# Twelve blocks of w2 in one half of the partitions and ten in the other: dealing the last MLP's units unevenly

## The chip, the cores and the metric

The kernel runs on one core of a Trainium2 chip. The metric is the device time of one execution in microseconds. A core has five engines that run side by side and wait for one another by semaphores: TensorE (PE; its weight loads are shown apart as PEld), VectorE (DVE), ScalarE (ACT), GpSimd (POOL) and SyncE (SP), which here issues nearly all transfers. Transfers between the chip's main memory and the on-chip memory of 128 partitions are carried out by 16 DMA engines.

## What is computed

One decoding step of a small transformer, in float32: two layers, each an attention block over a cache and an MLP, with the same weights and caches in both.

```python
def _A_ref(x, k_cache, v_cache, wq, wo):       # H=32 heads, Sk=4096, Dh=128, D=512
    q = (x @ wq).reshape(B, Sq, H, Dh).transpose(0, 2, 1, 3)
    scores = jnp.einsum("bhqd,bhkd->bhqk", q, k_cache) * (Dh ** -0.5)
    p = _softmax(scores, axis=-1)
    o = jnp.einsum("bhqk,bhkd->bhqd", p, v_cache)
    return o.transpose(0, 2, 1, 3).reshape(B, Sq, H * Dh) @ wo

def _B_ref(x, w1, b1, w2, b2):                 # D=512, F=1376
    h = _gelu(jnp.einsum("bsd,df->bsf", x, w1) + b1)
    return jnp.einsum("bsf,fd->bsd", h, w2) + b2

x = A_x
x = x + _A_ref(_layernorm(x), A_k_cache, A_v_cache, A_wq, A_wo)
x = x + _B_ref(_layernorm(x), B_w1, B_b1, B_w2, B_b2)
x = x + _A_ref(_layernorm(x), A_k_cache, A_v_cache, A_wq, A_wo)
x = x + _B_ref(_layernorm(x), B_w1, B_b1, B_w2, B_b2)
```

There is one token (B = Sq = 1). Every weight and both caches have to be read from main memory, 286 MB in all, and each element is used once a layer.

## The kernel before

**Storage.** One large tile, `arena` (L71), holds all weights and cache pieces. It is cut by hand into three regions for K or V of one group (`RING`, `A_AT`, `B_AT`, `C_AT`, L37) and some smaller places. `U` is 512 columns, `NC` 2,048. The heads are worked off in eight groups (`G`) of four. A group's K and V are 8 blocks of `NC` columns each, 8 MB each.

**Order of the work.** Layer one takes the groups 0 to 7 (loop at L417), layer two takes them backwards (L514). For each group, `blocks` (L353) issues the load of K, PE takes the scores, `exponentials` and `weights` make the softmax, V is loaded and multiplied. In the groups before the last, PE multiplies the first three blocks of V and `weighted` (L261) lets DVE multiply the other five and add them up in a tree (L265 and L270), in place, in columns 12U to 32U of the region that holds V. The tree's second addition (L270, 128x2048) is the last to read columns 20U to 24U.

**Queues.** All loads are issued by SP through `load` (L105), which keeps them in program order: an issue that has to wait for its place to become free, or for an earlier transfer's semaphore, holds those behind it. PE's matmuls are kept in program order as well (L110).

**The end.** The last group (L514 with `final`) has its V in region B. While it is worked on, region A, which held V of the group before, takes the MLP's weights. SP issues, in this order: V in four pieces (`LAST`, L53), the last quarter of wo (L528), w1 in three pieces (`W1_AT_END`, L52) to A_AT, and w2 in four pieces (`W2_AT_END`, L55: blocks 0 to 3, 4 to 7, 8 and 9, 10) to A_AT + 11U. Then `head_out` multiplies by wo and `mlp` (L307) does the rest.

**The MLP.** The 1,376 hidden units are dealt to four strips of 32 partitions, 344 each (`FJ`). For each chunk `c` of the input, four matmuls, one a strip, multiply by w1 (L310 to L313) into the PSUM tile `pO`. A few small steps take the norm. `idle(pS)` (L322) is a matmul whose result is not used, but for zeroing. DVE transposes `pO` in 32 x 32 squares (L324), so that the units stand in the partitions: strip j's unit 32 c + q comes to partition 32 j + q, column c. There are `FB` = 11 such columns, the last padded with zeros. Then come the GELU's steps (L326 to L333) on 11 columns, and for each column c four matmuls multiply block c of w2 (512 columns, 128 partitions) and add up in `pS` (L334 to L337). After one more transpose and addition SP stores the output (L538). Layer one's MLP is the same function, with its own order of w2's loads (`load_w2`, `behind_w2`). The bias b1 comes with a small transfer at the start, on ACT's queue (L131).

Of the kernel before, what the change touches and what calls it, by code (L numbers as in the profile page):

```python
# [14 lines left out]
ALU = mybir.AluOpType  # L15
AX = mybir.AxisListType

P = 128
# [4 lines left out]
J = 4  # L23
C = 8
FJ = F // J
FB = 11
W1C = FJ * J
EPS = 1e-5
U = 512
# [8 lines left out]
A_AT, B_AT, C_AT = RING  # L38
KEPT_V = 26 * U
SHARED = B_AT + KEPT_V  # L40
SCRATCH = SHARED + 10 * U
# [10 lines left out]
W1_AT_END = ((0, 2), (2, 3), (3, 4))  # L52
LAST = ((0, 4), (4, 6), (6, 7), (7, 8))  # L53
W2_AT_CHANGE = ((0, 2), (2, 5), (5, 8), (8, 10), (10, 11))
W2_AT_END = ((0, 4), (4, 8), (8, 10), (10, 11))  # L55


@with_exitstack
def decode_layers(ctx: ExitStack, tc: tile.TileContext, vectors, k, v, w, w1, w2, out):
    nc = tc.nc  # L60
    const = ctx.enter_context(tc.tile_pool(name="const", bufs=1))
    psum = ctx.enter_context(tc.tile_pool(name="psum", bufs=1, space=bass.MemoryType.PSUM))
# [19 lines left out]
    def small(name, n=1):  # L82
        nonlocal first_front, rest
        if name.startswith("gelu_"):
            i = "huaztg".index(name[-1])
            return cells[:, gelu + FB * i : gelu + FB * (i + 1)]
        if name not in places:
            fit = [j for j in range(J) if gaps[j] + n <= ends[j]]
            if name == "by_dma":
                places[name] = front, first_front, n  # L90
                first_front += n
            elif fit:
                places[name] = cells, gaps[fit[0]], n
                gaps[fit[0]] += n
            else:
                places[name] = cells, rest, n
                rest += n
        t, a, m = places[name]
        assert m == n and first_front <= FRONT and rest <= CELLS
        return t[:, a : a + n]  # L100

    def at(first, n):
        return arena[:, first : first + n]

    def load(first, src):  # L105
        t = at(first, src.shape[-1])
        tc.keep_in_program_order(nc.sync.dma_start(t, src))  # L107
        return t

    def matmul(*a, **kw):  # L110
        tc.keep_in_program_order(nc.tensor.matmul(*a, **kw))  # L111
# [4 lines left out]
    def part(src, g, a, b):  # L116
        return src[g][:, NC * a : NC * b]

    def of_w(row, i, n):
        return w[row][:, NC * i : NC * (i + n)]  # L120

    def by_four(t):
        return t.rearrange("p (j n) -> p j n", j=4)
# [6 lines left out]
    b1c, b2c, xcol = by_dma[:, :FB], by_dma[:, FB : FB + 4], by_dma[:, FB + 4 :]  # L130
# [12 lines left out]
    pS, pO = (psum.tile([P, 512], F32, name=n) for n in ("pS", "pO"))  # L143
# [10 lines left out]
    def of_32(t, n, i=0):  # L154
        return t[:, : 32 * n].rearrange("p (c q) -> p c q", q=32)[:, :, i]
# [4 lines left out]
    def pairs(t):  # L160
        return t[:, :8].rearrange("p (c i) -> p c i", i=2)
# [32 lines left out]
    def mean_of(xs, s):  # L194
        nm = minus_mean(s, pS[:, 0:1])
        xc, sq, ss, negm = small("xc", 4), small("sq", 4), small("ss"), small("negm")
        nc.vector.tensor_scalar(xc, pairs(xs)[:, :, 0], nm, None, op0=ALU.add)
        nc.vector.scalar_tensor_tensor(sq, xc, 1.0, xc, op0=ALU.mult, op1=ALU.mult, accum_out=ss)
        nc.vector.tensor_copy(negm, nm)
        return negm, ss  # L200

    def rstd_of(ss):
        nv = minus_mean(ss, pS[:, 1:2])
        ve, r = small("ve"), small("rstd")
        nc.vector.tensor_scalar(ve, nv, -1.0, EPS, op0=ALU.mult, op1=ALU.add)
        nc.vector.memset(pS[:, 0:2], 0.0)
        nc.gpsimd.tensor_tensor(r, ve, power, op=ALU.pow)
        return r
# [95 lines left out]
            else:  # L304
                matmul(to, on[:, d : d + P], wt[:, d, :], start=(d == 0), stop=(d == 3))

    def mlp(xs, s, w1_t, w2_t, load_w2=None, behind_w2=None):  # L307
        xb = small("xb", 4)
        nc.gpsimd.tensor_tensor(xb, pairs(xs)[:, :, 0], b2c, op=ALU.add)
        for c in range(4):  # L310
            for j in range(J):
                matmul(pO[32 * j : 32 * j + 2, :FJ], pairs(xs)[:, c, :], w1_t[c][:, FJ * j : FJ * (j + 1)],
                       start=(c == 0), stop=(c == 3))  # L313
            if c == 0:
                nm, ss = mean_of(xs, s)
            if c == 1:
                r = rstd_of(ss)
            if load_w2:
                load_w2(c)
                for _ in range(min(c + 1, 2) if c < 3 else 0):  # L320
                    idle(pO[:, 3 * P :], P, amid=True)
        idle(pS)  # L322
        ht = at(SCRATCH, 32 * FB)
        nc.vector.transpose(ht, pO[:, : 32 * FB])  # L324
        h, u, a, z, t, g = (small(f"gelu_{i}", FB) for i in "huaztg")
        nc.vector.scalar_tensor_tensor(h, of_32(ht, FB, 1), nm, of_32(ht, FB), op0=ALU.mult, op1=ALU.add)  # L326
        if load_w2:
            load_w2(4)
        nc.vector.scalar_tensor_tensor(u, h, r, b1c, op0=ALU.mult, op1=ALU.add)
        nc.vector.scalar_tensor_tensor(a, u, 0.044715, u, op0=ALU.mult, op1=ALU.mult)  # L330
        nc.vector.scalar_tensor_tensor(z, a, 1.0, u, op0=ALU.add, op1=ALU.mult)
        nc.scalar.activation(t, z, AF.Tanh, scale=float(np.sqrt(2.0 / np.pi)))
        nc.vector.scalar_tensor_tensor(g, t, 1.0, u, op0=ALU.add, op1=ALU.mult)  # L333
        for c in range(FB):  # L334
            for j in range(J):
                matmul(pS[32 * j : 32 * j + 1, :P], g[:, c : c + 1], w2_t[c][:, P * j : P * (j + 1)],
                       start=(c == 0), stop=(c == FB - 1))  # L337
            if load_w2:
                behind_w2(c)
                if c in (4, 7, FB - 1):  # L340
                    idle(pO, U // 2)
        return of_32(turned(pS), 4), xb

    def load_w1(first, a, b):
        load(first + W1C * a, w1[:, W1C * a : W1C * b])

    def load_w2(first, a, b):
        load(first + U * a, w2[:, U * a : U * b])

    def in_rows(first, n, rows):  # L350
        return [at(first + n * i, n) for i in range(rows)]

    def blocks(src, g, home, pieces=((0, C),)):  # L353
        for a, b in pieces:
            load(home + NC * a, part(src, g, a, b))
            for c in range(a, b):
                yield c, quarters(home + NC * c)

    xs, s = set_x(zero, 1.0, xcol)
# [54 lines left out]
    negm, z, sc, nsc = first_queries(xs, s, wq_t, wide=True)  # L414
    acc = pairs(xs)[:, :, 0]
    ahead = None
    for g in range(G):  # L417
        final = g == G - 1
        k_home, v_home = RING[2 * g % 3], RING[(2 * g + 1) % 3]
# [4 lines left out]
        if g < G - 2:  # L424
            t = partly(pt, blocks(v, g, v_home), v_home)
            pair = load(PAIR, of_w(g % 2, g, 2))
            ahead = t, rl, by_four(pair[:, :NC])
            z = next_queries(xs, negm, by_four(pair[:, NC:]), to=pS)
            continue
        for c, t in blocks(v, g, v_home, LAST if final else ((0, C),)):  # L430
# [3 lines left out]
            if g == G - 2:  # L434
                for j in range(J):
                    i = 4 * c + j - KEPT_V // U
                    if i >= 0:
                        nc.scalar.copy(pK[i], t[j])
        if final:
# [3 lines left out]
            own = head_out(rl, wo_t, last=True, home=ident)  # L443
            load_w1(SHARED, 3, 4)
        else:
# [3 lines left out]
            z = next_queries(xs, negm, wq_t)  # L449
    x1, s1 = set_x(own, 1.0, acc, queries=False)  # L450
# [9 lines left out]
    def behind_w2(c):  # L460
# [4 lines left out]
        if c == 9:  # L465
            begin_k(SHARED + 2 * NC, 2)

    own, xb = mlp(x1, s1, in_rows(SHARED, W1C, 4), in_rows(SHARED, U, FB),
                  lambda i: load_w2(SHARED, *W2_AT_CHANGE[i]), behind_w2)
    xs, s = set_x(own, 0.5, xb)  # L470

# [3 lines left out]
    g = G - 2  # L475
    negm, z, sc, nsc = first_queries(xs, s, wq_t)
# [22 lines left out]
    v_t = [at(B_AT + U * i, U) for i in range(KEPT_V // U)]  # L499
    for i, first in enumerate([SHARED, SHARED + U] + [PAIR + U * j for j in range(4)]):  # L500
        t = at(first, U)
# [8 lines left out]
    z = next_queries(xs, negm, by_four(pair[:, :NC]))  # L510
# [3 lines left out]
    for n in range(2, G):  # L514
        g, final = G - 1 - n, n == G - 1
        k_home, v_home = homes[(2 * n - 1) % 3], homes[2 * n % 3]
        acc, pt, rl = group(z, acc, ahead, blocks(k, g, k_home, HALVES if final else ((0, C),)))
        if not final:
            t = partly(pt, blocks(v, g, v_home, ((0, 6), (6, 8)) if n == 2 else ((0, C),)), v_home)
            pair = load(PAIR, of_w(g % 2, g - 1, 2))  # L520
            ahead = t, rl, by_four(pair[:, NC:])
            z = next_queries(xs, negm, by_four(pair[:, :NC]), to=pS)
            continue
        for c, t in blocks(v, g, v_home, LAST):
            values(c, pt, t, c)
            if c in (5, 7):
                idle(pS)
        wo_t = by_four(load(PAIR, of_w(g % 2, g, 1)))  # L528
        for a, b in W1_AT_END:
            load_w1(A_AT, a, b)  # L530
        for a, b in W2_AT_END:
            load_w2(A_AT + 11 * U, a, b)
        own = head_out(rl, wo_t, last=True)
    x1, s1 = set_x(own, 1.0, acc, queries=False)
    own, xb = mlp(x1, s1, in_rows(A_AT, W1C, 4), in_rows(A_AT + 11 * U, U, FB))
    y = small("y", 4)
    nc.vector.scalar_tensor_tensor(y, own, 0.5, xb, op0=ALU.mult, op1=ALU.add)
    nc.sync.dma_start(out, y)  # L538
# [2 lines left out]
def columns(a):  # L541

    return np.ascontiguousarray(a.reshape(J, 4, 32, -1).transpose(0, 2, 1, 3).reshape(P, 4, -1))
# [36 lines left out]
```

## Time and profile before

| | before |
|---|---|
| median of 3 runs | 673.12 us (673.02 to 673.5) |
| profiled run | 673.93 us, its span 672.1 us |
| mean granted TensorE clock | 0.794 |
| PE busy | 400.7 us (60% of the span) |
| DVE busy | 329.1 us (49%) |
| moved by DMA | 285.98 MB, mean 425 GB/s |

The span runs from the first to the last event of the program in the profile; the run's own time has a little more around it. A profile is one execution. In its rows, "idle before <- releaser" tells how long an engine had stood still and what ended that. A DMA share of 1 is all 16 engines at work; it can read a little above 1 where neighbouring packets overlap. PE's clock is granted by a throttle, 1.00 or 0.50. A matmul in float32 is recorded as two instructions. For an issued transfer the time "to landing" runs from the issue on SP to the last increment of its semaphore.

### The profile page before, as it was taken

The page shows a single profiled execution, that of the slowest core. Times are in us where ns is not written, and L with a number is a line of the kernel's source. Part 1 is how long each engine was busy: PE and PEld are TensorE (multiplying, and loading weights), DVE is VectorE, ACT ScalarE, POOL GpSimd, SP SyncE. Part 2 cuts the span into 40 slices and gives each one's busy share as a digit, 9 for nine tenths or more (in the row PEclk, how much of TensorE's full clock was granted, in tenths as well). Part 3 has the DMA queues.
Part 4 walks back from the last instruction along what each step waited for, and adds up shares of the span by engine and source line. Part 5 has one row for each costly group of instructions (what it writes and reads, how often), then busy time and mean ns, then how long its engine had stood idle before and what let it go on. Part 6 is the DMA issues. An engine that isn't in the chain of part 4 may idle for free. (4 is left out here: it accounts for less than half of the span.)

```text
span 672.1 us, 5792 instructions
## 1 busy us (share of the span) xinstructions
PE 400.7 (60%) x2470; PEld 109.8 (16%) x2470; DVE 329.1 (49%) x480; ACT 22.8 (3%) x48; POOL 4.9 (1%) x23
## 2 busy tenths in 40 slices
PE   4543753647616556376767878728527466275685
PEld 1110210111201111011214222102102111021122
DVE  2059276393682945921121221492772936928521
ACT  0010000000000000002000110000000000000000
POOL 0000000000000000000000000000000000000000
PEclk9956765976769767677989999877758867687698
DMA  9999999999999999999999999999999999999996
GB/s 375 437 437 437 438 430 437 414 456 437 437 434 410 459 434 437 433 434 395 433 423 393 426 452 421 437 435 434 437 433 409 458 434 430 437 426 419 435 420 257
DMA packets 11258, 285.98 MB, mean 425 GB/s; under 512 B 1505, under 2 KB 1505, under 8 KB 3297
## 3 DMA queue, kind: packets, MB, share of 16 engines
q1 hardware_dynamic: 11088, 285.61, 98.9%
q8 instruction: 19, 0.31, 0.2%
q14 instruction: 7, 0.05, 0.0%
q10 hardware_dynamic: 144, 0.01, 0.0%
HBM read 285.62 MB, written 0.00 MB: 425 GB/s over the span
## 5 line engine op out<-in xcount | busy, mean ns | idle before, releaser
L111 PE MATMUL pO<-arena,cells 128*128 128x512 f32 (+4 forms) x376 | 93.0, 606 | 145.5 <-DVE arena L270 127.7
L111 PE MATMUL pS<-arena,front 128*8 128x512 f32 x1036 | 146.4, 706 | 32.8 <-DMA arena<-in_k 29.1
L265 DVE TENSOR_TENSOR arena<-arena 128x10240 f32<-128x10240 f32 x11 | 119.1, 10825 | 32.0 <-DMA arena<-in_v 31.8
L111 PE MATMUL pO<-arena 128*4 128x512 f32 x584 | 94.7, 806 | 44.7 <-DMA arena<-in_v 42.9
L270 DVE TENSOR_TENSOR arena<-arena 128x2048 f32<-128x2048 f32 (+1 forms) x33 | 98.5, 2985 | 0.7
L228 DVE TENSOR_REDUCE cells<-pS 128x1 f32<-128x512 f32 x16 | 11.1, 692 | 152.1 <-PE pS L111 152.1
L111 PEld LDWEIGHTS pO<-arena,cells 128*128 128x128 f32 (+3 forms) x376 | 28.2, 122 | 195.1 <-DVE arena L270 136.8
L111 PEld LDWEIGHTS pS<-arena,front 128*8 128x8 f32 x1036 | 31.4, 101 | 154.0 <-issue 110.3
L111 PE MATMUL pS<-arena,cells 128*1 128x128 f32 (+1 forms) x328 | 50.5, 384 | 8.5 <-DMA arena<-in_w 7.0
L280 DVE STREAM_TRANSPOSE arena<-pO 128x512 f32<-128x512 f32 x16 | 11.5, 717 | 54.1 <-PE pO L111 54.1
L242 PE MATMUL pO<-front,arena 128*128 128x128 f32 x64 | 12.8, 333 | 36.9 <-ACT arena L237 36.9
L111 PEld LDWEIGHTS pO<-arena 128*4 128x4 f32 x584 | 16.2, 102 | 107.7 <-issue 99.8
L169 DVE STREAM_TRANSPOSE arena<-pO 32x128 f32<-32x128 f32 x64 | 19.9, 311 | 20.1 <-PE pO L111 19.1
L237 ACT ACTIVATE arena<-pS,cells 128x512 f32<-128x512 f32 x16 | 12.4, 778 | 502.8 <-DVE cells L233 502.8
L111 PEld LDWEIGHTS pS<-arena,cells 128*1 128x1 f32 (+1 forms) x328 | 21.9, 118 | 45.2 <-issue 36.4
L231 DVE TENSOR_REDUCE cells<-cells 128x1 f32<-128x8 f32 x16 | 2.6, 161 | 29.4 <-PE pO L111 29.2
L242 PEld LDWEIGHTS pO<-front,arena 128*128 128x128 f32 x64 | 8.1, 161 | 49.9 <-ACT arena L237 48.8
L169 DVE STREAM_TRANSPOSE arena<-pS 32x128 f32<-32x128 f32 x44 | 13.7, 310 | 0.8
L171 DVE STREAM_TRANSPOSE arena<-pS 128x128 f32<-128x128 f32 x3 | 1.0, 317 | 12.7 <-PE pS L111 12.7
L247 DVE STREAM_TRANSPOSE cells<-cells 128x32 f32<-128x32 f32 x16 | 3.4, 214 | 7.0 <-ACT arena L237 5.9
L384 DVE MEMSET pS<- 128x512 f32 x11 | 5.3, 485 | 1.2
L245 DVE COPY arena<-pO 128x128 f32<-128x128 f32 x16 | 4.5, 284 | 1.4 <-PE pO L242 1.1
(63 smaller groups left out, 73.6 us busy)
## 6 DMA issues: line engine op xcount, KB each, us to landing
arena<-in_w SPq DMA_DIRECT2D x13, 2048.0 KB, 11.5
arena<-in_k SPq DMA_DIRECT2D x4, 4096.0 KB, 25.1
arena<-in_v SPq DMA_DIRECT2D x2, 4096.0 KB, 38.9
arena<-in_w SPq DMA_DIRECT2D x6, 1024.0 KB, 21.4
arena<-in_v SPq DMA_DIRECT2D x3, 2048.0 KB, 43.0
arena<-in_v SPq DMA_DIRECT2D x1, 6144.0 KB, 30.8
arena<-in_w SPq DMA_DIRECT2D x6, 688.0 KB, 30.3
arena<-in_v SPq DMA_DIRECT2D x4, 1024.0 KB, 46.2
```

What stands on the lines that cost most here:

```text
L111: tc.keep_in_program_order(nc.tensor.matmul(*a, **kw))
L169: nc.vector.transpose(t[q], src[q, P * j : P * (j + 1)])
L228: nc.vector.tensor_reduce(ml[:, 0:1], pS, axis=AX.X, op=ALU.max)
L231: nc.vector.tensor_reduce(m, mt[:, :C], axis=AX.X, op=ALU.max)
L237: nc.scalar.activation(p, pS, AF.Exp, bias=bias[:, 0:1], scale=sc, accum_out=ml[:, 0:1])
L242: tc.keep_in_program_order(nc.tensor.transpose(pT[:, b].rearrange("p j r -> p (j r)"), p[:, P * b : P * (b + 1)], ident))
L245: nc.vector.tensor_copy(pt, pT[:, :, :, :C].rearrange("p b j c -> p c j b"))
L247: nc.vector.transpose(lt, ml)
L265: nc.vector.tensor_tensor(t, t, w.unsqueeze(2).to_broadcast([P, 4 * J * (C - BY_PE), P]), op=ALU.mult)
L270: nc.vector.tensor_tensor(a, a, b, op=ALU.add)
L280: nc.vector.transpose(ot, pO)
L384: nc.vector.memset(pS, 0.0)
```

## The change

It touches the last MLP only; layer one's MLP is called with values that leave it as it was.

- The units are dealt 384, 384, 304 and 304 to the four strips (`UNITS_AT_END`). After the transpose the partitions under 64 have twelve columns of units, the others nine and a half, padded to ten. A second copy of w2, `w2_at_end`, is laid out for that, with twelve blocks a row; blocks 10 and 11 are loaded and multiplied for the partitions under 64 alone.
- All 128 partitions load blocks 0 to 9, in four pieces (0 to 3, 4 to 6, 7 and 8, 9). Blocks 10 and 11 of the lower 64 partitions come in eight transfers of eight rows, four partitions apart (3, 7, ... 31, say), 4,096 bytes a row, 32 KB a transfer. Three of them are issued between and behind the pieces of V, one behind wo, three behind w1's pieces and one behind w2's first piece.
- w2's blocks are multiplied in the order 10, 11, 0, 1, ... 9, and for 10 and 11 with 64 rows.
- w1 gets 64 columns in front, of which the first twelve hold b1 in the new dealing; so it comes with w1's first piece.
- The GELU's small arrays lie in region A of the arena, not in `cells`, and have twelve columns.

```diff
-W2_AT_END = ((0, 4), (4, 8), (8, 10), (10, 11))
+W2_AT_END = ((0, 4), (4, 7), (7, 9), (9, 10))
+UNITS_AT_END = (384, 384, 304, 304)
+FB_AT_END, FB_BOTH = 12, 10
+HEAD = 64
...
-    def mlp(xs, s, w1_t, w2_t, load_w2=None, behind_w2=None):
+    def mlp(xs, s, w1_t, w2_t, units, n, b1c, gelu_at, load_w2=None, behind_w2=None):
...
-                matmul(pO[32 * j : 32 * j + 2, :FJ], pairs(xs)[:, c, :], w1_t[c][:, FJ * j : FJ * (j + 1)],
+                a = sum(units[:j])
+                matmul(pO[32 * j : 32 * j + 2, : units[j]], pairs(xs)[:, c, :], w1_t[c][:, a : a + units[j]],
                        start=(c == 0), stop=(c == 3))
...
-        for c in range(FB):
+        first = 0 if load_w2 else FB_BOTH
+        for i in range(n):
+            c = (first + i) % n
+            rows = w2_t[c].shape[0]
             for j in range(J):
-                matmul(pS[32 * j : 32 * j + 1, :P], g[:, c : c + 1], w2_t[c][:, P * j : P * (j + 1)],
-                       start=(c == 0), stop=(c == FB - 1))
+                matmul(pS[32 * j : 32 * j + 1, :P], g[:rows, c : c + 1], w2_t[c][:, P * j : P * (j + 1)],
+                       start=(i == 0), stop=(i == n - 1))
...
+    def load_w2_at_end(first, a, b, rows=slice(P)):
+        tc.keep_in_program_order(nc.sync.dma_start(at(first + U * a, U * (b - a))[rows],
+                                                   w2_at_end[rows, U * a : U * b]))
...
-        for c, t in blocks(v, g, v_home, LAST):
+        w1_home, w2_home = A_AT + HEAD, A_AT + 11 * U
+        eights = [slice(r, r + 29, 4) for r in (0, 32, 1, 33, 2, 34, 3, 35)]
+
+        def load_eight():
+            load_w2_at_end(w2_home, FB_BOTH, FB_AT_END, eights.pop())
+
+        v_t = []
+        for a, b in LAST:
+            v_t += blocks(v, g, v_home, ((a, b),))
+            if a:
+                load_eight()
+        for c, t in v_t:
             values(c, pt, t, c)
...
         wo_t = by_four(load(PAIR, of_w(g % 2, g, 1)))
+        load_eight()
         for a, b in W1_AT_END:
-            load_w1(A_AT, a, b)
-        for a, b in W2_AT_END:
-            load_w2(A_AT + 11 * U, a, b)
+            if a:
+                load_w1(w1_home, a, b)
+            else:
+                load(A_AT, w1[:, : HEAD + W1C * b])
+            load_eight()
+        load_w2_at_end(w2_home, *W2_AT_END[0])
+        load_eight()
+        for a, b in W2_AT_END[1:]:
+            load_w2_at_end(w2_home, a, b)
...
-    own, xb = mlp(x1, s1, in_rows(A_AT, W1C, 4), in_rows(A_AT + 11 * U, U, FB))
+    w2_t = in_rows(w2_home, U, FB_AT_END)
+    w2_t[FB_BOTH:] = [t[: P // 2] for t in w2_t[FB_BOTH:]]
+    own, xb = mlp(x1, s1, in_rows(w1_home, W1C, 4), w2_t, UNITS_AT_END, FB_AT_END, at(A_AT, FB_AT_END),
+                  lambda i, n: at(A_AT + 25 * U + 16 * i, n))
```

More of the change, by code (lines that the diff above doesn't have):

```diff
@@ L54, with decode_layers @@
 W2_AT_CHANGE = ((0, 2), (2, 5), (5, 8), (8, 10), (10, 11))
-W2_AT_END = ((0, 4), (4, 8), (8, 10), (10, 11))
+W2_AT_END = ((0, 4), (4, 7), (7, 9), (9, 10))
+UNITS_AT_END = (384, 384, 304, 304)
+FB_AT_END, FB_BOTH = 12, 10
+HEAD = 64
 @with_exitstack
-def decode_layers(ctx: ExitStack, tc: tile.TileContext, vectors, k, v, w, w1, w2, out):
+def decode_layers(ctx: ExitStack, tc: tile.TileContext, vectors, k, v, w, w1, w2, w2_at_end, out):
     nc = tc.nc
@@ L322, in mlp @@
         idle(pS)
[L323 to L326, printed above, removed]
+        ht = at(SCRATCH, 32 * n)
+        nc.vector.transpose(ht, pO[:, : 32 * n])
+        h, u, a, z, t, g = (gelu_at(i, n) for i in range(6))
+        nc.vector.scalar_tensor_tensor(h, of_32(ht, n, 1), nm, of_32(ht, n), op0=ALU.mult, op1=ALU.add)
         if load_w2:
@@ L344, in load_w1 @@
     def load_w1(first, a, b):
-        load(first + W1C * a, w1[:, W1C * a : W1C * b])
+        load(first + W1C * a, w1[:, HEAD + W1C * a : HEAD + W1C * b])
     def load_w2(first, a, b):
         load(first + U * a, w2[:, U * a : U * b])
+    def load_w2_at_end(first, a, b, rows=slice(P)):
+        tc.keep_in_program_order(nc.sync.dma_start(at(first + U * a, U * (b - a))[rows],
+                                                   w2_at_end[rows, U * a : U * b]))
     def in_rows(first, n, rows):
@@ L466, in behind_w2 @@
             begin_k(SHARED + 2 * NC, 2)
-    own, xb = mlp(x1, s1, in_rows(SHARED, W1C, 4), in_rows(SHARED, U, FB),
+    own, xb = mlp(x1, s1, in_rows(SHARED, W1C, 4), in_rows(SHARED, U, FB), (FJ,) * J, FB, b1c,
+                  lambda i, n: small(f"gelu_{'huaztg'[i]}", n),
                   lambda i: load_w2(SHARED, *W2_AT_CHANGE[i]), behind_w2)
@@ L551 @@
     b1 = np.pad(a["b1"].reshape(J, FJ), ((0, 0), (0, pad)))
+    starts = np.cumsum((0,) + UNITS_AT_END[:-1])
+    w2_at_end, b1_at_end = (np.stack([np.pad(t[i : i + n], ((0, 32 * FB_AT_END - n), (0, 0))) for i, n in
+                                      zip(starts, UNITS_AT_END)]).reshape(J, FB_AT_END, 32, -1).transpose(0, 2, 1, 3)
+                            .reshape(P, -1) for t in (a["w2"], a["b1"].reshape(-1, 1)))
     wq = columns(a["wq"]).reshape(P, 4, G, J, J, 32)
@@ L565 @@
         w=apart(np.array(w).transpose(0, 2, 1, 3).reshape(2, P, G * NC)),
-        w1=columns(a["w1"]).reshape(P, 4 * J * FJ),
+        w1=np.concatenate((np.pad(b1_at_end, ((0, 0), (0, HEAD - FB_AT_END))),
+                           columns(a["w1"]).reshape(P, 4 * J * FJ)), axis=1),
         w2=w2.reshape(J, FB, 32, D).transpose(0, 2, 1, 3).reshape(P, FB * D),
+        w2_at_end=w2_at_end,
     )
```

## The prediction

> **What bounds the kernel now.** I began with the page, for the engine that is never idle.
>
> ```profile
> span 672.1 us, 5792 instructions
> PE 400.7 (60%) x2470; PEld 109.8 (16%) x2470; DVE 329.1 (49%) x480; ACT 22.8 (3%) x48; POOL 4.9 (1%) x23
> DMA  9999999999999999999999999999999999999996
> q1 hardware_dynamic: 11088, 285.61, 98.9%
> q8 instruction: 19, 0.31, 0.2%
> ```
>
> The 16 DMA engines are busy in every slice of the span but the last, and 98.9% of their time goes to the loads that SP issues. No compute engine is above 60%. So only two things can move the end: the bytes that the latest DMA engine has to carry, and the work that follows its last byte. The chain of waits, read at its end, says the same:
>
> ```profile
> 646.71 20.18 DMA arena<-in_w
> 666.90 0.04 issue
> 666.94 2.28 PE pS L111 x56
> 669.25 0.33 DVE arena L171
> 669.60 0.16 DVE cells L537
> ```
>
> The w2 blocks 4 to 7 land at 666.9; PE then multiplies blocks 4 to 10 as they come. The change is all about these last microseconds, so I asked for the engines' busy time in stretches of the tail (columns: stretch, its length, busy time of five engines, granted TensorE clock, DMA share, GB/s).
>
> ```profile
> 657.00:659.00 2.00, 1.65 (x36) 0.67 (x40) 0.47 (x6) 0.00 (x0) 0.20 (x1) 1.00 1.03 430
> 665.50:665.75 0.25, 0.25 (x12) 0.19 (x8) 0.00 (x0) 0.00 (x0) 0.00 (x0) 0.50 0.54 213
> 665.75:666.00 0.25, 0.25 (x12) 0.17 (x8) 0.00 (x0) 0.00 (x0) 0.00 (x0) 0.50 0.43 172
> 666.50:667.00 0.50, 0.06 (x4) 0.06 (x8) 0.00 (x0) 0.00 (x0) 0.00 (x0) 0.50 0.17 66
> 667.00:668.50 1.50, 1.50 (x44) 1.09 (x48) 0.00 (x0) 0.00 (x0) 0.00 (x0) 0.71 0.06 22
> ```
>
> This is the finding on which everything rests. The 16 engines do not finish together: about half have nothing left at 665.75 (share 0.54, then 0.43), some three of 16 work on at 666.5 to 667.0 (0.17), and from 667.0 to 668.5 a single one does (0.06 is 1/16). The kernel waits some 3 us for one straggler after half of the engines are done. What held it up shows in the DMA queues of one microsecond:
>
> ```profile
> q8 instruction: 1, 0.02, 5.6%
> ```
>
> That is the stretch 662.25 to 663.30. One fetch of instructions, 16 KB, took 5.6% of 16 engines over 1.05 us, so 0.94 us of one engine. [...]
>
> **The change part by part.** *Bytes.* A w2 block is 512 floats in each partition, 2,048 bytes. An engine carries, by the even share, eight partitions' rows: 16,384 bytes a block, at 430/16 = 26.9 GB/s (first stretch above) 0.61 us. Eleven blocks everywhere become twelve and ten, so the total is the same and, if the two halves of the partitions belong to two sets of eight engines, one set ends 0.61 us later and the other 0.61 us earlier. The 64 columns ahead of w1 add 128 x 256 bytes = 32 KB, 0.08 us on all engines. The last transfer therefore ends 0.53 us earlier if the straggler serves partitions from 64 on, 0.69 us later if it serves those below, and 0.08 us later if the eight-row transfers spread over all 16.
>
> No view names the engine behind a packet, so no row decides between the halves. [...] I take the upper half as the likelier place of the straggler; that is a judgment without a row behind it, and it is the weakest step of this prediction.
>
> *The queue.* Eight more issues go on SP, and the first stands ahead of two pieces of V.
>
> ```profile
> L107 SPq DMA_DIRECT2D arena<-in_v x2: 432/432/432, 603.1 to 603.6; - x2
> DMA to landing us min/median/max: 43.5/44.5/45.5
> 623.29 2.23 DVE L270 TENSOR_TENSOR arena<-arena 128x2048 f32<-128x2048 f32 x1
> L107 SPq DMA_DIRECT2D arena<-in_w x1: 328/328/328, 646.7 to 646.7; - x1
> DMA to landing us min/median/max: 20.2/20.2/20.2
> L107 SPq DMA_DIRECT2D arena<-in_w x1: 328/328/328, 649.1 to 649.1; - x1
> DMA to landing us min/median/max: 19.1/19.1/19.1
> L107 SPq DMA_DIRECT2D arena<-in_w x1: 328/328/328, 651.5 to 651.5; - x1
> DMA to landing us min/median/max: 17.2/17.2/17.2
> out<-cells SPq DMA_DIRECT2D x1, 2.0 KB, 1.4
> ```
>
> The two extra blocks go to columns that the tree of sums of the group before still reads until 625.5 (623.29 + 2.23). So SP stands from about 604 to 625.5 with V's last two pieces, wo and the weights behind it. What hides this: V's piece before lands at 603.1 + 43.5 = 646.6, so the DMA engines have 21 us of work queued at 625.5. Cost 0; without that cover up to 22 us.
>
> The issues at 646.7 and 649.1 fall on landings of V pieces (603.1 + 43.5, 603.6 + 45.5): each issue waits for the one eight places before it, so eight are in flight at most. With the small ones between, the eight hold fewer bytes. w2's second piece would go when w1's first has landed, near 657; ahead of it then are 688 + 688 + 1,024 KB, 5.7 us at 430. If the eight-row transfers also wait for one another in pairs, it goes near 659 with some 3.5 us ahead. A lone transfer's whole trip is 1.4 us (last row). So no engine that matters runs dry: 0 on both readings.
>
> What each small transfer costs its engines: one row of 4,096 bytes, 0.15 us, already in the 0.61 x 2. A fixed price would show between neighbours in the queue. The last two w2 pieces land at 649.1 + 19.1 = 668.2 and 651.5 + 17.2 = 668.7, 0.5 us apart for 256 KB that need 0.61 at 430. So I take 0; the other bound is the lone trip, 1.4 us each.
>
> *Compute.* These rows of the timeline carry it:
>
> ```profile
> 655.38 1.06 PE L111 MATMUL pS<-arena,cells 128*1 128x128 f32 x32 [0.26 <-DVE cells L286]
> 660.63 0.76 PE L111 MATMUL pO<-arena,cells 128*2 128x344 f32 x8 [0.96 <-DMA arena<-in_w]
> 661.46 0.55 DVE L324 STREAM_TRANSPOSE arena<-pO 128x352 f32<-128x352 f32 x1 [2.12 <-PE pO L111]
> 663.38 0.17 DVE L333 SCALAR_TENSOR_TENSOR cells<-cells 128x11 f32<-128x11 f32 x1 [0.34 <-ACT cells L332]
> 664.60 1.89 PE L111 MATMUL pS<-arena,cells 128*1 128x128 f32 x32 [2.16 <-DMA arena<-in_w]
> 666.94 2.24 PE L111 MATMUL pS<-arena,cells 128*1 128x128 f32 x56 [0.45 <-DMA arena<-in_w]
> ```
>
> The w1 matmuls widen from 344 to 384 columns in two of four strips: 0.76 x 384/344 = 0.85, +0.09 on the last chunk. The transpose goes from 352 to 384 columns, +0.05. The GELU's last step ends at 663.55 and w2 is awaited until 664.6, so 1.0 us of slack covers both, and the 11 to 12 columns of the small steps. The GELU's inputs move from one tile to another, at no cost. b1 comes with w1's first piece, which PE waits for anyway.
>
> w2's matmul records go from 88 to 96. The eight blocks' worth of waiting moves too: blocks 10 and 11 go first, and the last of them lands behind w2's first piece on the lower engines only, which are early in this case; 16 records, before or just beside the wait for 664.6. What follows is blocks 4 to 9 in 48 records against seven blocks in 56. Straggler in the upper half: first piece 664.65, second (three blocks, 1.83) 666.5, third 667.7, last 668.2. PE at the half clock of the 664.60 row takes 1.89/32 = 59 ns a record, at full clock 1.06/32 = 33. Twenty-four records from 666.5 end at 667.9 at the half clock; then 16 and 8 end at 668.4 and 668.7 at full clock, at 669.3 if the clock stays at half. Before, PE ended at 669.18. So the 0.53 us arrives whole at full clock and not at all at half. The clock read 0.50 until 667 and 0.71 over 667.0 to 668.5, so most of that stretch was at full clock; I take 0.5.
>
> **Sum.** -0.61 + 0.08 = -0.53, of which 0.5 reaches the end. The profiled run had a span of 672.1 and 673.93 with what lies around it, 0.8 above the median 673.12. So span 671.6, profiled 673.4, median **672.6**. No more than 0.1% either way: 0.2%, 1.35 us, is about what a measurement of this kernel can tell from no change.
>
> **Rivals.** *The straggler serves the lower half*: +0.69 on the last landing, nothing of it hidden, 673.8. For it: no row names the engine. Against it: only the judgment above.
>
> *The shift meets nothing*: the eight-row transfers spread over all 16 engines, or PE's half clock eats the gain: 673.0 to 673.3. For it: the 0.50 clock through 667.
>
> *Slower, each small transfer holds its engines*: with x us extra each, the lower engines, half of them done by 665.75, end at 665.75 + 0.69 + 8x. It decides from x = 0.22 (past 668.2) and passes 0.2% from x = 0.46. At the lone trip's 1.4 less 0.15, 8 x 1.25 = 10 us: 676.4 against 668.7, some 681. Against it: the 0.5 us between neighbours. [...]
>
> *Faster by more*: the fetch at 662.3 moves off the straggler. The next-latest engine is done near 667.2, so the end would fall by some 2 us to 671.1. Against it: PE's instructions up to there keep their number.
>
> **How the numbers follow.** Upper half 0.52, lower half 0.22, nothing 0.16, held engines 0.05, moved fetch 0.05. The first three, 0.9, span 672.6 to 673.8; with the spread of the runs before (0.5) the range is 672.0 to 673.9. The first case alone: 672.4 to 673.1. Faster by over 0.2% is the last case and the outermost of the first, 0.06; slower the held engines and a little of the second, 0.06; within, 0.88.
>
> **What would show it.** Right: the DMA share of the last 1.5 us again at 0.06, but ending near 668.0; PE's last w2 records behind the last landing; SP's issues of V's last two pieces at 625.5, and no hole in the DMA row before 664. Wrong: the lone engine works to 669 or later (lower half); a share of 0.5 in the tail, eight engines late together (held engines); PE without a DMA wait after w2's second piece (clock); a DMA row below 9 before the tail (dry queue).

## The result and the profile after

The changed kernel takes 684.81 us (median of 5 runs, 683.75 to 685.54); the kernel before took 673.12 beside it (5 runs, 672.78 to 674.58). The ratio is 1.0167, with an interval of 1.0151 to 1.0183: 11.7 us slower, where 0.5 us less was forecast and 673.9 was the end of the range. One execution of those below, of 839.33 us in the fourth experiment, lay far off the others and is left out; all other times compare like with like. The profiled run is the 683.75 one, with a span of 681.9 at a mean granted clock of 0.787 (0.794 before).

The page of the kernel after, in the parts that the prediction began with: busy time, the DMA row of the slices, and the main queue.

```profile
span 681.9 us, 5820 instructions
PE 399.5 (59%) x2478; PEld 110.3 (16%) x2478; DVE 329.3 (48%) x480; ACT 22.8 (3%) x48; POOL 4.9 (1%) x23
DMA  9999999999999999999999999999999999999991
q1 hardware_dynamic: 11216, 285.65, 97.6%
```

The engines work about as long as before: PE 399.5 us against 400.7, DVE 329.3 against 329.1. The bytes are nearly the same (285.65 MB against 285.61), only the span around them is longer, and the last slice is nearly empty (1 where it was 6). So the kernel now ends with some 12 us in which little is transferred. A slice is 17 us long, though; a short hole doesn't show in it. Shorter stretches of the kernel after (columns as in the prediction's table of stretches):

```profile
642.00:644.00 2.00, 0.66 (x4) 0.42 (x4) 1.71 (x9) 0.73 (x2) 0.00 (x0) 1.00 0.96 410
644.00:646.00 2.00, 1.99 (x12) 0.45 (x16) 0.03 (x1) 0.00 (x0) 0.00 (x0) 0.55 0.60 180
646.00:648.00 2.00, 2.00 (x16) 0.45 (x12) 0.00 (x0) 0.00 (x0) 0.00 (x0) 0.60 0.81 299
657.00:659.00 2.00, 0.00 (x0) 0.00 (x0) 0.00 (x0) 0.00 (x0) 0.00 (x0) 0.71 0.95 393
667.00:668.50 1.50, 1.22 (x24) 0.51 (x16) 0.22 (x1) 0.00 (x0) 0.00 (x0) 0.50 0.68 269
668.50:669.50 1.00, 0.59 (x7) 0.26 (x11) 0.27 (x3) 0.00 (x0) 0.20 (x1) 0.50 0.07 27
```

Two things are new. From 644 to 648 the DMA engines stand still for a part of the time: 2 x 0.40 + 2 x 0.19 = 1.2 us. And from 657 to 659 PE, DVE, ACT and POOL do nothing at all, while the weights go on landing until about 669.4, only 0.7 us later than before (668.7). What holds up the transfers shows in SP's own timeline and in SP's waits (us in total, times, longest):

```profile
602.52 0.90 SPq L112 DMA_DIRECT2D arena<-in_v  x2
643.99 0.78 SPq L360 DMA_DIRECT2D arena<-in_w_at_end  x1
644.81 0.40 SPq L112 DMA_DIRECT2D arena<-in_v  x1
645.26 0.66 SPq L360 DMA_DIRECT2D arena<-in_w_at_end  x1
```

```profile
SPq L360 <- DVE cells L256: 36.7, 1, 36.7
```

The first eight-row transfer (L360) goes out at 643.99, not at the forecast 625.5, and V's last two pieces, wo, w1 and w2 queue up behind it. What holds up the compute engines shows in the timeline of the last head and the MLP. The first fence is one row of the kernel before, the second the kernel after.

```profile
654.88 0.18 DVE L284 TENSOR_REDUCE cells<-arena 128x4 f32<-128x16 f32 x1
```

```profile
654.22 0.72 DVE L285 STREAM_TRANSPOSE arena<-pO 128x512 f32<-128x512 f32 x1 [10.19 <-PE pO L116]
665.83 0.18 DVE L289 TENSOR_REDUCE cells<-arena 128x4 f32<-128x16 f32 x1 [10.89 <-DMA arena<-in_w_at_end]
666.33 1.89 PE L116 MATMUL pS<-arena,cells 128*1 128x128 f32 x32 [11.12 <-DVE cells L291]
668.91 1.45 PE L116 MATMUL pO<-arena,cells 128*2 128x384 f32 x8 [0.69 <-issue]
673.10 0.58 DVE L330 STREAM_TRANSPOSE arena<-pO 128x384 f32<-128x384 f32 x1 [0.99 <-PE pO L116]
675.21 2.91 PE L116 MATMUL pS<-arena 64*1 64x128 f32 x96 [1.14 <-DVE arena L339]
678.72 0.35 SPq L574 DMA_DIRECT2D out<-cells  x1
```

The reduction of the last head's output (L289, L284 before) has its input at 654.94. Before, it followed at once; now it stands 10.89 us, and the releaser is a transfer of the extra w2 blocks. So wo's product starts at 666.33 instead of 655.38, and the whole MLP (w1, transpose, GELU, all 96 records of w2) comes after the weights instead of beside their landing. From the reduction to the end of the span it is 16.1 us in one row.

Neither wait follows from data. L289 reads columns 51,200 to 51,683 of the arena, and the eight-row transfers write columns 10,752 to 11,775. The view of L360 names the one that L289 waits for: issued at 656.1, the last of the eight. The first of them goes out 0.03 us after the end of the copy that writes the last softmax's transposed weights (L250, columns 50,688 to 50,815), where the tree's second addition would do; the view of the waits names L256, that softmax's last instruction, but L256 ends at 644.02, after the issue at 643.99.

```profile
643.67 0.29 DVE L250 COPY arena<-pO 128x128 f32<-128x128 f32 x1
643.87 0.15 DVE L256 RECIPROCAL cells<-cells 128x1 f32<-128x1 f32 x1
```

Both transfers and instructions are in one tile, and the transfer's rows are four partitions apart. From that comes the theory that the experiments start from, an assumption so far: it takes the spaced rows and the shared tile together to bring these two waits, which the data doesn't need.

### The profile page after: what moved, and what is told of

Its sections match the earlier page's. It is cut to its first block, busy times and chain, and to the rows that moved or that the text cites. A ratio compares the mean times of both kernels' runs of the same rounds, so it can differ in the third digit from the quotient of the medians.

```text
span 681.9 us, 5820 instructions
## 1 busy us (share of the span) xinstructions
PE 399.5 (59%) x2478; PEld 110.3 (16%) x2478; DVE 329.3 (48%) x480; ACT 22.8 (3%) x48; POOL 4.9 (1%) x23
## 3 DMA queue, kind: packets, MB, share of 16 engines
q1 hardware_dynamic: 11216, 285.65, 97.6%
HBM read 285.65 MB, written 0.00 MB: 419 GB/s over the span
## 5 line engine op out<-in xcount | busy, mean ns | idle before, releaser
L116 PE MATMUL pO<-arena,cells 128*128 128x512 f32 (+6 forms) x376 | 94.2, 618 | 144.4 <-DVE arena L275 127.8
L116 PE MATMUL pS<-arena,cells 128*1 128x128 f32 (+1 forms) x240 | 46.6, 412 | 17.9 <-DVE cells L291 11.1
L116 PEld LDWEIGHTS pO<-arena 128*4 128x4 f32 x584 | 16.1, 101 | 107.4 <-issue 100.3
L116 PEld LDWEIGHTS pS<-arena,cells 128*1 128x1 f32 (+1 forms) x240 | 19.4, 126 | 52.0 <-issue 33.9
L289 DVE TENSOR_REDUCE cells<-arena 128x4 f32<-128x16 f32 x16 | 2.9, 181 | 11.4 <-DMA arena<-in_w_at_end 10.9
## 6 DMA issues: line engine op xcount, KB each, us to landing
arena<-in_w SPq DMA_DIRECT2D x13, 2048.0 KB, 11.7
```

The lines of the kernel that those rows point to most:

```text
L289: nc.vector.tensor_reduce(o, own, axis=AX.X, op=ALU.add)
```

## The experiments

In all rows below "before" is the kernel before, run on the same chip.

**Neighbouring rows.** The eight rows of a transfer lie side by side; everything else stays.

```diff
-        eights = [slice(r, r + 29, 4) for r in (0, 32, 1, 33, 2, 34, 3, 35)]
+        eights = [slice(r, r + 8) for r in (0, 32, 8, 40, 16, 48, 24, 56)]
```

> The changed kernel with one edit: the eight small transfers take eight neighbouring rows each, not rows four apart; same rows in all, same bytes, same order. Theory (the step of four rows makes the scheduler unable to tell these writes from other uses of the arena, so SP's first small issue waits for a softmax copy at 644 and DVE's reduction of the last head waits for the last small transfer, 10.9 us): both waits go, the reduction starts near 655 and SP issues the first one near 625.5; time 672.6 if the straggling DMA engine serves the upper half, 673.8 if the lower. Rival (each small transfer holds its eight DMA engines some 1.2 us): no change, 683 to 685.

Measured: 675.49 against 673.38 before, ratio 1.0027 (1.0017 to 1.0038). 9.3 of the 11.7 us are gone. SP's first small issue, the reduction, and two stretches of this kernel:

```profile
625.79 0.35 SPq L360 DMA_DIRECT2D arena<-in_w_at_end  x1
```

```profile
654.98 0.18 DVE L289 TENSOR_REDUCE cells<-arena 128x4 f32<-128x16 f32 x1
```

```profile
657.00:660.00 3.00, 1.70 (x32) 0.72 (x32) 0.56 (x6) 0.00 (x0) 0.20 (x1) 1.00 1.07 370
660.00:663.00 3.00, 1.40 (x16) 0.22 (x16) 0.22 (x2) 0.00 (x0) 0.55 (x1) 1.00 0.97 370
```

Both waits are gone: the issue is at 625.79, and the reduction has no idle time in brackets. So it is the spacing of the rows that made them. But 2.1 us remain, and the last two rows show something else: the DMA engines are busy all the time and move 370 GB/s, where the prediction's stretch from 657 had 430.

**One wait at a time.** With the first four transfers spaced and the last four side by side, SP's wait should stay; the other way round, DVE's wait for the last ones should.

```diff
+        eights = [slice(r, r + 8) for r in (32, 40, 48, 56)] + [slice(r, r + 29, 4) for r in (0, 1, 2, 3)]
```

> The first four small transfers keep rows four apart (in rows 0 to 31), the last four take neighbouring rows (32 to 63). Theory: SP is still held at the first one until 644, so the DMA row keeps its hole at 644 to 648 and the last w2 piece lands near 669.4 as in the changed kernel, but DVE's reduction waits only for the fourth transfer, near 656; time 674.6. Rival (held engines): 683 to 685.

Measured: 677.38 against 673.38, ratio 1.0058 (1.0044 to 1.0071).

```profile
SPq L360 <- DVE cells L256: 37.9, 1, 37.9
```

```profile
644.00:646.00 2.00, 1.42 (x16) 0.54 (x19) 0.95 (x6) 0.00 (x0) 0.00 (x0) 1.00 0.23 98
646.00:648.00 2.00, 2.00 (x24) 0.47 (x20) 0.00 (x0) 0.00 (x0) 0.00 (x0) 1.00 0.63 131
```

```profile
656.95 0.18 DVE L289 TENSOR_REDUCE cells<-arena 128x4 f32<-128x16 f32 x1 [0.97 <-DMA arena<-in_w_at_end]
```

SP is held as in the changed kernel, the hole in the transfers (the idle share of both stretches) is 2 x 0.77 + 2 x 0.37 = 2.3 us deep, and the reduction waits 0.97 us only, for the last of the spaced four. The 4.0 us are this hole, part of the slow transfers of the neighbouring rows, and that short wait; this run doesn't part them, and they are 2.8 us more than was expected.

```diff
+        eights = [slice(r, r + 29, 4) for r in (0, 1, 2, 3)] + [slice(r, r + 8) for r in (32, 40, 48, 56)]
```

> The first four small transfers take neighbouring rows (32 to 63), the last four rows four apart (in 0 to 31). Theory: SP is free at 625.5 and the DMA row has no hole, but DVE's reduction waits for the eighth transfer, which lands near 663 behind w2's first piece; from there the changed kernel took 16.1 us to its end, so 679.4 span and 681.2 time. Rival (the hold on SP is the larger cause): 673 to 675. Rival (held engines): 683 to 685.

Measured: 682.78 against 673.38, ratio 1.0133 (1.0118 to 1.0149).

```profile
625.41 0.35 SPq L360 DMA_DIRECT2D arena<-in_w_at_end  x1
```

```profile
664.96 0.18 DVE L289 TENSOR_REDUCE cells<-arena 128x4 f32<-128x16 f32 x1 [10.41 <-DMA arena<-in_w_at_end]
```

Without the hold of SP the reduction still waits 10.41 us, and 9.4 of the 11.7 us are back, 1.6 more than expected (the eighth transfer landed near 665, not 663). This wait is the larger part. Both runs have four transfers of neighbouring rows; the first experiment puts eight of them, with the uneven dealing, at 2.1 us, so four cost about 1 in each run. 4.0 + 9.4 - 2 = 11.4, near the 11.7: an estimate, as the parts needn't add up.

**The small transfers without the dealing.** The kernel before, with eight transfers of eight neighbouring rows in the same places of the queue; what they load nobody reads. The code is cut: the row slices are those of the first experiment, the calls those of the changed kernel.

```diff
+        def load_eight():
+            rows = eights.pop()
+            tc.keep_in_program_order(nc.sync.dma_start(at(A_AT + 22 * U, 2 * U)[rows], w2[rows, : 2 * U]))
```

> The kernel before, units dealt evenly as there, plus eight transfers of eight neighbouring rows (32 KB each, columns that nothing reads, from w2's first two blocks) at the places in SP's order where the changed kernel has its small ones. It adds 0.6 x 2 = 1.2 us of load on the DMA engines that carry them and takes nothing from the others. Theory with the straggler among the engines that carry no small ones: 673.1 to 673.3. Straggler among those that carry them: 674.3. Rival (held engines): 681 to 684.

Measured: 676.5 (median of four) against 673.38, ratio 1.0044 (1.0031 to 1.0058), 3.1 us over it. Neither theory had this number: too much for the bytes alone, too little for transfers that hold their engines one by one.

```profile
657.00:660.00 3.00, 1.12 (x36) 0.74 (x32) 0.49 (x3) 0.00 (x0) 0.20 (x1) 0.99 1.01 367
```

367 GB/s at a share of 1.01, the same slow transfers as with neighbouring rows above, and here without the uneven dealing. So rows side by side seem to have a price of their own. To see the dealing itself, the rows have to stay four apart, and the two waits have to go in another way.

**Spaced rows without the waits.** The changed kernel, but the last softmax's transposed weights go to `ident` (no longer needed), and the last head's output is transposed into PSUM instead of the arena. Six PSUM tiles of 512 columns become three of 1,024. The main lines:

```diff
+        if aside:
+            turned_at[0] = ident
...
-        ot = at(SCRATCH, U)
+        ot = aside[0][:, :U] if aside else at(SCRATCH, U)
...
-        own = at(SCRATCH, 4 * 129).rearrange("p (b q) -> p b q", q=129)[:, :, :P]
+        own = aside[0][:, : 4 * 129] if aside else at(SCRATCH, 4 * 129)
...
+        if final:
+            aside.append(pK2[0])
```

> The changed kernel, rows four apart as in it, but with the two places moved out of the arena that the scheduler could not tell from the small transfers: the last softmax's transposed weights go to the tile that held the identity matrix, the last head's transposed sums to PSUM. Theory (the changed kernel's loss is the two false waits, and what was left with neighbouring rows is eight DMA engines writing the same few partitions at once): no hole in the DMA row, the last head's reduction near 655, and the uneven dealing shows by itself: 672.9 if the straggling engine carries no small transfers, 674.0 if it does. Rival (each small transfer costs its engines whatever its rows): 675.5, as with neighbouring rows.

Measured: 673.46 (11 runs) against 673.32 (27 runs), ratio 1.0010 (1.0000 to 1.0019).

```profile
625.19 0.78 SPq L365 DMA_DIRECT2D arena<-in_w_at_end  x1
```

```profile
654.25 0.18 DVE L294 TENSOR_REDUCE cells<-pK 128x4 f32<-128x16 f32 x1
```

```profile
657.00:660.00 3.00, 2.36 (x40) 0.83 (x40) 0.66 (x6) 0.00 (x0) 0.29 (x1) 1.00 1.03 430
```

No wait, 430 GB/s, and the whole loss is gone: the same eight transfers, the same uneven dealing, 11.3 us less. With the next run, that settles the cause of the slowdown: the two waits. Why the program has them isn't shown; what is shown is that they need both the spaced rows and the shared tile. The run also shows what the dealing is worth where nothing stands in its way: not a gain of 0.5 us, but between nothing and a loss of 1.3.

The two moves without the change, as a base:

> The kernel before with only those two places moved. Both are off the last transfer's path: 673.4 on both theories, as the kernel before.

Measured: 673.22, ratio 1.0003 (0.9993 to 1.0014). The moves alone make no difference that these runs can tell.

**Bytes or a price for each transfer.** To that base come the eight unread transfers again, now with rows four apart.

```diff
+        eights = [slice(r, r + 29, 4) for r in (0, 32, 1, 33, 2, 34, 3, 35)]
...
+            tc.keep_in_program_order(nc.sync.dma_start(at(A_AT + 22 * U, 2 * U)[rows], w2[rows, : 2 * U]))
```

> The kernel before with the two places moved, and eight small transfers that nothing reads, as in the earlier run with neighbouring rows (676.85), but with rows four apart. Theory (neighbouring rows collide, rows four apart do not): 673.4 to 673.6 if the straggling engine carries none of them, 674.6 if it does. Rival (they cost their engines whatever the rows): 676.9.

Measured: 674.28, ratio 1.0017 (1.0009 to 1.0026), 1.1 us over the base; with neighbouring rows the same eight cost 3.1 us over the kernel before.

```profile
657.00:660.00 3.00, 2.29 (x40) 0.67 (x40) 1.11 (x9) 0.00 (x0) 0.58 (x2) 1.00 1.04 431
```

431 GB/s with rows four apart, 367 with rows side by side. Then the same with rows twice as long (four blocks, 8,192 bytes) and with rows of 512 bytes:

> The kernel with the two moves and eight unread eight-row transfers, rows four apart, with rows of four blocks (8,192 bytes) instead of two; nobody reads what they load, so the output is untouched. With two blocks it stood 1.1 us over the kernel with the moves alone (674.28 against 673.22). If that was the bytes on the engines that carry them (eight rows a transfer at 26.9 GB/s an engine: 0.30 us each here, 2.4 in all), those engines hold the latest one already and the time is 673.2 + 2.4 = 675.6. If it was a price for each transfer, whatever it carries, 674.3 again. If the latest engine is one of the other eight and the bytes had first to use up its lead, the step from two blocks to four is the full 1.2 us (675.5) while the step from none to two was smaller: this run alone can't tell that from the first by less than its spread.

Measured: 675.93 against 673.39, ratio 1.0033 (1.0021 to 1.0046).

> The same eight transfers with rows of 128 columns (512 bytes): 0.02 us each by the bytes, 0.15 in all. If bytes are the cost, 673.2 + 0.2 = 673.4, no difference from the kernel with the moves alone. If each transfer costs its engines a price of its own, some 0.13 us (1.1 over eight), 674.3 as with two blocks. The prediction's rival of the held engines, at its lower bound of 0.22 us each, needs 675 or more here.

Measured: 673.81 against 673.39, ratio 1.0007 (0.9998 to 1.0017).

In us over before, by the ratios: 0.5 with 512 bytes a row (-0.1 to 1.1), 1.1 with 4,096 (0.6 to 1.8), 2.2 with 8,192 (1.4 to 3.1). By the bytes, if eight engines carry them, which no view shows, it should be 0.15, 1.2 and 2.4 (the estimate of the expectations, at 26.9 GB/s an engine), by a price for each transfer three times the same. One constant price doesn't fit: the first interval ends at 1.1 and the last begins at 1.4. So it is the bytes in the main. A small price beside them isn't excluded, up to 1.1 us for the eight or 0.14 us each. If all 16 engines shared them evenly, it should be half, and 1.2 is under the last interval. And as most of the estimated time arrives at the end (2.2 us of 2.4), the engines that carry the eight-row transfers have, by that estimate and in the mean of the runs, little lead over the latest one.

## Why the prediction was wrong

**The step that failed** is *The queue*, with its sentence "So SP stands from about 604 to 625.5" and "Cost 0". It took the last reader of the overwritten columns as what the issue waits for, which is what the data needs; in the run without waits, the first issue did go at 625.19. The program waits for more: SP until 643.99. The cover that the step counted on, transfers already queued, lasted nearly as long, so the hole was 1.2 us deep and not "up to 22 us". The larger part isn't in the prediction at all, which in effect put it at nothing: it looked for what SP waits for, and for PE's waits on the weights that it multiplies, never for a wait on the new transfers of an instruction that doesn't read them. The reduction at L289 got one, of 10.89 us. Its run alone gave 9.4 us, of which about 1 goes to neighbouring rows by the estimate above. The prediction named the sign, "a DMA row below 9 before the tail (dry queue)"; the row of slices stayed at 9 and only the stretches of 2 us showed it.

**Compute.** The 1.0 us of slack that was to cover w1 and the GELU was a right reading of the kernel before; the wait used it up ten times over. The wider transpose took 0.58 us instead of 0.55. w2's 96 records took 2.91 us in one go, 30 ns each, near the forecast 33 ns at full clock, but in another place. In the run without waits the granted clock is 1.00 from 663 to 668.5, so no half clock ate a gain there.

**Bytes and half.** That the total stays was right (285.65 MB against 285.61), and that some engines carry more fits what the unread transfers cost. The 0.61 us of the sum, and the 0.15 us of a small transfer in it, need each half of the partitions to have eight engines of its own, which no run shows; what the runs showed in their place is 1.1 us for eight unread transfers of 4,096 bytes a row, and no gain from the dealing. The half was judged wrongly: the run without waits has no gain and at most a small loss. The forecast gave 0.52 to the straggler among the engines that get less, without a row for it; the run without waits gave +0.10% (0.00 to 0.19) where that case has -0.08%. That leaves out the forecast's case, but it holds both the lower half's rival at +0.69 us, 0.10%, and the rival in which the shift meets nothing (up to 0.03%); against the base with the two moves, at 0.03% itself, the second is as near. Which came isn't shown, nor that an instruction fetch held the straggler, nor that the same engine is last in each execution. The range itself was a little tight: 673.8 with the spread of 0.5 ends at 674.3, not at 673.9.

**Held engines.** This rival's time, some 681, lies nearest to the measured 684.8 by luck; its mechanism is wrong. The same eight transfers without the two waits cost at most 1.3 us in all. With 512 bytes a row the eight transfers cost 0.07%, -0.1 to 1.1 us, where its own lower bound of 0.22 us a transfer means 1.8 us of engine time. In these runs, with transfers of 4 KB, 32 KB and 64 KB in a full queue, what the eight cost (0.5, 1.1 and 2.2 us) goes by the bytes in the main. The prediction's 0 for a fixed price stands to within 0.14 us a transfer.

**In flight.** The forecast that shorter transfers in the eight places starve no engine held: 430 and 427 GB/s from 657 to 663 in the run without waits.

```profile
660.00:663.00 3.00, 1.97 (x14) 0.41 (x10) 0.82 (x2) 0.00 (x0) 0.26 (x1) 1.00 1.02 427
```

## What to carry to other kernels

A transfer into a shared tile with spaced partitions can be ordered against instructions that touch quite other columns, as here, where the reduction stood 10.89 us and the first small issue went at 643.99 instead of 625.19: look at the waits that each new transfer gets, and at the waits that later instructions get on it, before costing its bytes. Where a wait makes no sense by the data, give the reader or the writer another tile, as the run without waits did, and the loss is gone, here 11.3 us. A dealing of bytes that is meant to relieve the latest of 16 engines needs a view that says which engine is the latest; without one it was here a bet of half a microsecond either way, by the prediction's estimate.

## What the runs showed of the hardware

In these runs eight rows side by side went with a lower rate of everything that was in flight: 367 and 370 GB/s at a full share from 657 to 660, against 430 and 431 with rows four partitions apart and the same bytes, and 3.1 us against 1.1 in time. Why isn't shown: no view names the engine behind a packet or the partitions that it writes, so the theory of eight engines that write the same few partitions at once stays a theory, and the rows' addresses in main memory change along with the partitions. Neighbouring rows can't be the only cause of a low rate either: the changed kernel has spaced rows alone, and behind the hole that SP's hold left it moved 369 GB/s at a full share (in the profile before, 424 over 648 to 657).

```profile
650.00:652.00 2.00, 2.00 (x14) 0.40 (x6) 0.00 (x0) 0.00 (x0) 0.00 (x0) 1.00 0.99 369
```

What slowed it there stays open.

Here an issue of spaced rows takes SP twice as long as one of rows side by side: 0.66 us in the changed kernel (the row at 645.26 above), 0.33 in the first experiment, here its second small issue.

```profile
626.57 0.33 SPq L360 DMA_DIRECT2D arena<-in_w_at_end  x1
```
